# Attention products with v cut into 64x32 tiles that sum in a spare half bank, scores packed on 640 columns, maxima issued ahead of the mask wait

## The chip, the cores and the metric

The kernel runs on one core of one Trainium2 chip. The metric is the device time of one execution in microseconds (us). The kernel before takes 1580.54 us, the median of 3 runs (1578.85 to 1582.73).

The engines are named as in the profile: PE is TensorE's matmul, PEld its weight load, DVE is VectorE, ACT is ScalarE, POOL is GpSimd, SP is SyncE (it issues most DMAs).

## The reference

Four layers are applied in turn to x (2048 rows of 640): attention, feed-forward, attention, feed-forward, with the same weights both times.

```python
def _A_ref(x, wqkv, wo):          # H = 32 heads, Dh = 20, window W = 256
    qkv = (x @ wqkv).reshape(B, S, 3, H, Dh).transpose(2, 0, 3, 1, 4)
    q, k, v = qkv
    scores = einsum("bhqd,bhkd->bhqk", q, k) * Dh ** -0.5
    mask = (i - j >= 0) & (i - j < 256)          # i query, j key
    p = softmax(where(mask, scores, -1e9))
    return einsum("bhqk,bhkd->bhqd", p, v) ... @ wo
def _B_ref(x, w1, b1, w2, b2):
    return relu(x @ w1 + b1) ** 2 @ w2 + b2
x = x + _A_ref(_layernorm(x)); x = x + _B_ref(_layernorm(x))     # twice
```

## The kernel before, in words

**Units.** The rows are cut into blocks of T = 256, so each of the 2 layers has 8 blocks; a block of a layer is a *unit* u, 16 in all. A query of a unit sees keys of its own block and of the one before it. Only units 0 and 8 (the first block of a layer) have no block before.

**Dense work.** The projections to q and k (`stage_qk`), to v (`stage_v`), the output projection (`stage_o`) and the feed-forward (`stage_f`) are chains of 128x128 matmuls, all issued on one line, L327. Every operand is split into two fp16 parts and three of the four products are summed. The moving operand has 256 columns (q, k, first feed-forward matrix) or 320 (v, output, second feed-forward matrix). They accumulate in two buffers of PSUM, `acc` (tag "mm").

**Attention work.** Heads go in groups of four, a *quad*: 8 quads per unit. The four heads of a quad are j = 0, 1 by e = 0, 1. For a quad three things happen on PE:

- *maxima* (`max_quad`, L653): the scores with queries on partitions, 38 matmuls on 64x64 tiles, into `bb`, two PSUM tensors of three banks of 512 columns (e = 0 is bb_133 in the built program, e = 1 is bb_134). They fill columns 0 to 1280 of the 1536. DVE then merges two window ends (COPY_PREDICATED, L666) and takes the row maximum (TENSOR_REDUCE, L669), once for each e. The maxima are turned, by a DMA, into extra rows of q, so that the second set of scores already has its row maximum subtracted.
- *scores* (`exp_quad`, L767): the scores again, keys on partitions, 32 matmuls on 64x64 tiles into the same `bb`. ACT takes their exponential into `pt` (L789), six times 512 columns. POOL sets what the window excludes to zero, eight affine_selects of 128x256 (L804, L808).
- *product with v* (`pv_quad`, L838): pt times v in fp32 on 128x32 tiles, so that the four heads of the quad run side by side, each on its 32 columns of PE; 16 matmuls, each of which the profile shows as two records (x32). A head streams 768 columns (256 + 128 + 128 + 256). The sum lies in an "mm" buffer, and ACT copies it to `ot` (L850), which is stored to DRAM by DMA.

The maxima of a quad run three quads ahead of its scores (LEAD). `bb` is one pair of buffers, so maxima wait for the exponentials that read the scores, and scores wait for the reduction that read the maxima.

**What sets the order.** Each engine runs its instructions in the order in which Python issues them. PE's order comes out of a small planner: it keeps a clock `now` with a cost for each piece of PE work, and a list of jobs for DVE, ACT, POOL and SP with costs and priorities (`urgency`, 0 first), issued when the planned clock gets there. In `together` (L1105 ff.) a unit alternates: scores of quad n, dense work, maxima of quad n + 3 and product of quad n, dense work. `work(part, Want(...))` issues dense work until its share is done and the jobs named in `Want` have ended by the plan. Before the maxima, `Want` names the exponentials and the first masks of quad n (`wants += quad[1][0]`, L1146); then the maxima and the product follow each other directly.

Where a buffer is written and read by different engines, semaphores are set when the program is built. The planner does not know them.

In the steady units (2 to 7 and 9 to 13) the order of PE repeats from unit to unit. `stage_o` of the last unit must wait until the last product has gone to DRAM and come back (`load_o`, `od`); the planner keeps feed-forward work of the unit before for that time (KEEP, CARRY).

Of the kernel before, what the change touches and what calls it, by code (L numbers as in the profile page):

```python
# [45 lines left out]
def kernel(ctx: ExitStack, tc: tile.TileContext, x, wqkv, wo, w1, b1, w2, b2, out):  # L46
# [12 lines left out]
    masks = sb.tile([P, 3 * P], BF16, name="pt", tag="pt", bufs=6)  # L59
# [120 lines left out]
    class Want:  # L180
        def __init__(self, *jobs, bank=True):
            self.jobs, self.bank = [j for j in jobs if j is not None], bank

    def when(w):

        if any(j.end is None for j in w.jobs):
            return None
        t = max([0.0] + [j.end for j in w.jobs])
        if w.bank and len(banks2) > 1:
            free = [max(j.end for j in b) + LAT for b in banks2 if b and all(j.end is not None for j in b)]  # L190
            if not free:
                return None
            t = max(t, min(free))
        return t
# [125 lines left out]
    urgency = {"out": 0, "turn": 1}  # L320
# [134 lines left out]
    def ln_cross(u, *deps):  # L455

        prio = 1 if u == 3 else 2
# [288 lines left out]

    def exp_quad(n):

        u, qd = divmod(n, NQ)
        qt = qts[u]  # L750
        bb = banks()
        whole = not quarters(u) or n == NQ
        steps = steps_of(u)
        if qd % GQ == 0:
            need(rowjobs.pop((u, qd // GQ)))
        pieces = []
        for k, st in enumerate(steps):
            o = 0
            for kb, kt, ko, q0, qn in st:
                w = qn * P  # L760
                for j in range(2):
                    for h in range(0 if whole else 2):
                        a, b = (0, w - 64 * (1 - h)) if kb < 2 else (64 * h, w)

                        def put(e, k=k, kt=kt, ko=ko, q0=q0, j=j, h=h, o=o, a=a, b=b):
                            r, rows = slice(64 * e, 64 * e + 3 * DH + 2), slice(64 * h, 64 * (h + 1))
                            nc.tensor.matmul(bb[e][rows, k, o + a:o + b],  # L767
                                             kt[r, 2 * qd + j, ko + 64 * h:ko + 64 * (h + 1)],
                                             qt[r, 2 * qd + j, q0 * P + a:q0 * P + b], start=True, stop=True,
                                             tile_position=(64 * e, 64 * h))  # L770

                        pieces.append((h, b - a, put))
                    for e in range(2 if whole else 0):
                        r = slice(64 * e, 64 * e + 3 * DH + 2)
                        nc.tensor.matmul(bb[e][:, k, o:o + w], kt[r, 2 * qd + j, ko:ko + P],  # L775
                                         qt[r, 2 * qd + j, q0 * P:q0 * P + w], start=True, stop=True)
                    o += w
        by_tiles(pieces)
        now[0] += (870.0 if whole else 763.0) if u % NG else 530.0
        out, masks = [], []  # L780
        for k, st in enumerate(steps):
            pts, ms = [], []
            for e in range(2):
                o = sum(2 * qn * P for _, _, _, _, qn in st)
                box = {}

                def power(k=k, e=e, o=o, box=box):
                    box["pt"] = sb.tile([P, 512], F32, name="pt", tag="pt", bufs=6)
                    nc.scalar.activation(box["pt"][:, :o], bb[e][:, k, :o], AF.Exp, scale=SCALE / (QS * QS))  # L789

                ex = post("A", 50 + 0.834 * o, power, prio=urgency["turn"])
                bbjobs.append(ex)
                o2 = 0
                for kb, kt, ko, q0, qn in st:
                    w = qn * P
                    part = slice(o2, o2 + 2 * w)
                    o2 += 2 * w

                    def mask(box=box, part=part, kb=kb, w=w):
                        pj = box["pt"][:, part].rearrange("p (j n) -> p j n", j=2)  # L800
                        if kb < 2:

                            m = pj[:, :, w - P:w]
                            nc.gpsimd.affine_select(out=m, in_=m, pattern=[[0, 2], [-1, P]],  # L804
                                                    compare_op=ALU.is_gt, fill=0.0, base=0, channel_multiplier=1)
                        else:
                            m = pj[:, :, 0:P]
                            nc.gpsimd.affine_select(out=m, in_=m, pattern=[[0, 2], [1, P]],  # L808
                                                    compare_op=ALU.is_ge, fill=0.0, base=0, channel_multiplier=-1)

                    ms.append(post("G", 375, mask, ex, prio=0 if n > NQ * NU - 4 else 1))
                    pts.append((e, kb, q0, qn, box, part))
            out.append(pts)
            masks.append(ms)
        return out, masks

    def steps_of(u):

        cur, prev = kts[u % 3], kts[(u - 1) % 3]
        if u % NG == 0:  # L820
            return [[(2, cur, 0, 0, 2)], [(3, cur, P, 1, 1)]]
        return [[(1, prev, P, 0, 2)], [(0, prev, 0, 0, 1), (3, cur, P, 1, 1)], [(2, cur, 0, 0, 2)]]

    def pv_quad(n, quad):
        u, qd = divmod(n, NQ)
        steps = steps_of(u)
        pv, jobs = mm_tile([P, T], "pv")
        for k, pts in enumerate(quad[0]):
            need(*quad[1][k])
            for kb, kt, ko, q0, qn in steps[k]:  # L830
                vf = vts[(2 * (u if kb >= 2 else u - 1) + kb % 2) % 6][1]
                for j in range(2):
                    for e, kb_, _, _, box, part in pts:
                        if kb_ == kb:
                            jj = 2 * j + e
                            c = (4 * qd + jj) * (DH + 1)
                            pj = box["pt"][:, part].rearrange("p (j n) -> p j n", j=2)
                            nc.tensor.matmul(pv[32 * jj:32 * (jj + 1), q0 * P:(q0 + qn) * P],  # L838
                                             vf[:, c:c + 32], pj[:, j, :], start=(k == 0),
                                             stop=(k == len(steps) - 1), skip_group_check=True,  # L840
                                             tile_position=(0, 32 * jj))
            now[0] += 480.0 if u % NG else 400.0
# [6 lines left out]
        def out():  # L849
            nc.scalar.copy(ot[:, qd % 2], pv)  # L850
# [6 lines left out]
        jobs.append(post("A", 262, out, prio=0))  # L857
        if qd % 2:
            ojobs[u, qd] = dma(write, 4 * (DH + 1) * 2 * T * 4, jobs[-1], n=4, cost=350.0)
# [5 lines left out]
    ols = {}  # L865

    def load_o(u, late=False, free_=()):
# [42 lines left out]
        for i in range(4):  # L910
# [15 lines left out]
            pr = 2 if u else 1  # L926
# [4 lines left out]
        ols[u] = od, x1, js, xj  # L931
        if u == 0:
# [371 lines left out]
```

## Time and profile before

| | us |
|---|---|
| median of 3 runs | 1580.54 |
| the profiled execution, its own time | 1585.88 |
| its span, first to last instruction | 1584.2 |
| PE busy | 1555.0 |
| DVE busy | 928.6 |
| ACT busy | 733.5 |
| POOL busy | 607.9 |

The profile is of one execution. A row of groups reads: line, engine, operation, output<-input, partitions x elements, count | busy time, mean ns of one | idle time before it and what ended it. A row of the timeline reads: start (us from the start of the span), length, engine, line, operation, count, and in brackets the idle time before it and its releaser. Lengths of matmul records are modelled and overlap; the difference between two starts is what counts.

### The profile page before, as it was taken

The numbers are of one execution on the slowest core, as the hardware profiler recorded it, in microseconds if no ns is written. First come the engines' busy times: TensorE is split into PE (matmuls) and PEld (weight loads), VectorE is DVE, ScalarE is ACT, GpSimd is POOL, SyncE is SP. The second block draws the span as 40 slices with busy tenths as digits, with TensorE's granted clock in tenths as the row PEclk, the third lists the DMA queues.
The fourth block names the chain that finished last, engine by engine and source line by source line (L and its number), as shares of the span: only waits on it lengthen the run. The fifth ranks groups of instructions, "written<-read, shape, count | busy, mean of one in ns | idle before, by whom it ended". The sixth has DMA issues, their size and how long they took to land.

```text
span 1584.2 us, 51151 instructions
## 1 busy us (share of the span) xinstructions
PE 1555.0 (98%) x21570; PEld 1167.1 (74%) x21570; DVE 928.6 (59%) x1910; ACT 733.5 (46%) x1593; POOL 607.9 (38%) x1291
## 2 busy tenths in 40 slices
PE   8888999999999999999999999999999999999999
PEld 7665778777777777777777777777777777777777
DVE  8776664565655566465465646566465565556542
ACT  4454545345354444534434454444534445445522
POOL 1232535335343352534414253343524435344522
PEclk9999999999999999999999999999999999999999
DMA  9764343352534625345253533525344253441120
GB/s 270 192 175 125 69 116 83 98 115 65 121 80 108 122 50 123 87 106 108 62 138 81 117 91 107 111 54 120 86 120 94 67 132 68 123 90 58 30 65 19
DMA packets 243341, 160.35 MB, mean 101 GB/s; under 512 B 91176, under 2 KB 226856, under 8 KB 243112
## 3 DMA queue, kind: packets, MB, share of 16 engines
q1 hardware_dynamic: 236744, 147.58, 38.6%
q10 hardware_dynamic: 6368, 9.50, 2.0%
q8 instruction: 169, 2.77, 0.8%
q14 instruction: 60, 0.49, 0.1%
HBM read 84.68 MB, written 52.95 MB: 87 GB/s over the span
## 4 chain that ended last, share of the span: by engine, by line
PE 93%; DVE 2%; DMA 2%; ACT 1%; issue 1%; POOL 0%; SPq 0%; ACTq 0%; DVEq 0%; POOLq 0%
PE acc L327 72%; PE pv L838 11%; PE bb L653 5%; PE bb L767 5%; ACT pt L789 1%; DMA x<-in_A_x_dram 1%; PE bb L775 0%; DMA qt<-mT 0%; DVE mx L669 0%; PE bb L678 0%; DVE bb L633 0%; DMA o<-ot 0%; DVE bst L353 0%; DMA xt<-in_A_x_dram 0%; DVE bb L666 0%
## 5 line engine op out<-in xcount | busy, mean ns | idle before, releaser
L789 ACT ACTIVATE pt<-bb 128x512 f32<-128x512 f32 (+1 forms) x736 | 374.0, 600 | 226.0 <-PE bb L767 198.8
L804 POOL TENSOR_SCALAR_AFFINE_SELECT pt<-pt 128x256 f32<-128x256 f32 x448 | 187.2, 420 | 539.7 <-ACT pt L789 525.6
L327 PE MATMUL acc<-y,w_s 128*128 128x256 f16 x2880 | 328.3, 273 | 0.1
L327 PE MATMUL acc<-w_s,hh 128*128 128x320 f16 (+1 forms) x2340 | 326.8, 298 | 0.0
L327 PEld LDWEIGHTS <-w_s 128*128 128x128 f16 x2880 | 276.5, 98 | 51.3 <-issue 15.0
L327 PEld LDWEIGHTS <-hh 128*128 128x128 f16 x2340 | 221.9, 98 | 97.6 <-issue 12.7
L669 DVE TENSOR_REDUCE mx<-bb 128x4 f32<-128x1024 f32 x224 | 273.9, 1223 | 6.6
L327 PEld LDWEIGHTS <-wq_s 128*128 128x128 f16 x2400 | 230.1, 98 | 46.8 <-issue 14.0
L327 PE MATMUL acc<-yT,wq_s 128*128 128x256 f16 x2250 | 258.8, 273 | 2.3 <-DVE qd L510 0.9
L808 POOL TENSOR_SCALAR_AFFINE_SELECT pt<-pt 128x256 f32<-128x256 f32 x512 | 223.1, 458 | 92.3 <-ACT pt L789 91.0
L1023 DVE TENSOR_TENSOR hh<-r,hh 128x256 f16<-128x256 f32 x192 | 94.6, 516 | 225.1 <-ACT hh L1020 218.2
L838 PE MATMUL pv<-pt,vt 128*32 128x128 f32 (+1 forms) x3840 | 189.5, 330 | 0.2 <-POOL pt L804 0.2
L850 ACT COPY ot<-pv 128x256 f32<-128x256 f32 x128 | 47.6, 372 | 286.2 <-PE pv L838 286.2
L1017 POOL TENSOR_TENSOR r<-r 128x256 f32<-128x256 f32 x192 | 114.2, 616 | 157.9 <-ACT r L1013 155.9
L666 DVE COPY_PREDICATED bb<-maskq,bb 128x256 f32<-128x256 uint16 x224 | 93.3, 423 | 98.6 <-PE bb L653 96.8
L327 PE MATMUL acc<-wo_s,od 128*128 128x320 f16 x960 | 140.5, 302 | 3.4 <-DVE od L924 1.9
L838 PEld LDWEIGHTS pv<-pt,vt 128*32 128x32 f32 x3840 | 104.8, 109 | 40.1 <-POOL pt L808 5.5
L327 PE MATMUL acc<-wq_s,yT 128*128 128x320 f16 x900 | 130.6, 300 | 1.4 <-DVE y L378 0.9
L327 PEld LDWEIGHTS <-od 128*128 128x128 f16 x960 | 91.8, 98 | 48.6 <-issue 6.4
L1013 ACT ACTIVATE r<-acc,b1s 128x256 f32<-128x256 f32 x192 | 80.5, 471 | 85.8 <-PE acc L327 84.7
L327 PEld LDWEIGHTS <-yT 128*128 128x128 f16 x900 | 85.5, 98 | 40.7 <-issue 7.8
L364 POOL TENSOR_TENSOR bmv<-bmv,neghalf 128x1 f32<-128x1 f32 x64 | 45.2, 712 | 156.0 <-DVE bmv L358 155.5
(96 smaller groups left out, 1241.6 us busy)
## 6 DMA issues: line engine op xcount, KB each, us to landing
qt<-qk SPq DMA_DIRECT2D x30, 480.0 KB
kt<-qk SPq DMA_DIRECT2D x30, 480.0 KB
qk<-qd SPq DMA_DIRECT2D x17, 640.0 KB
o<-ot SPq DMA_DIRECT2D x256, 42.0 KB
od<-o SPq DMA_DIRECT2D x14, 640.0 KB
qk<-yl SPq DMA_DIRECT2D x13, 640.0 KB
qk<-qd SPq DMA_DIRECT2D x17, 320.0 KB
xt<-in_A_x_dram SPq DMA_DIRECT2D x16, 320.0 KB
```

The source lines that it names most:

```text
L327: nc.tensor.matmul(acc, lhs(a, c), rhs(b, c), start=(k == 0), stop=(k == 3 * nk - 1))
L653: nc.tensor.matmul(flat[e][rows, o:o + b - a], qt[r, p, i * P + 64 * h:i * P + 64 * (h + 1)], kt[r, p, a + to:b + to], start=True, stop=Tr ...
L666: nc.vector.copy_predicated(wins[:, :, 4 * Q:], later, wins[:, :, :Q])
L669: nc.vector.tensor_reduce(most, wins[:, :, Q:], axis=mybir.AxisListType.X, op=ALU.max)
L767: nc.tensor.matmul(bb[e][rows, k, o + a:o + b], kt[r, 2 * qd + j, ko + 64 * h:ko + 64 * (h + 1)], qt[r, 2 * qd + j, q0 * P + a:q0 * P + b] ...
L789: nc.scalar.activation(box["pt"][:, :o], bb[e][:, k, :o], AF.Exp, scale=SCALE / (QS * QS))
L804: nc.gpsimd.affine_select(out=m, in_=m, pattern=[[0, 2], [-1, P]], compare_op=ALU.is_gt, fill=0.0, base=0, channel_multiplier=1)
L808: nc.gpsimd.affine_select(out=m, in_=m, pattern=[[0, 2], [1, P]], compare_op=ALU.is_ge, fill=0.0, base=0, channel_multiplier=-1)
L838: nc.tensor.matmul(pv[32 * jj:32 * (jj + 1), q0 * P:(q0 + qn) * P], vf[:, c:c + 32], pj[:, j, :], start=(k == 0), stop=(k == len(steps) - ...
L1013: nc.scalar.activation(box["r"], acc[:, f, :], AF.Relu, bias=b1s[:, f0 + f:f0 + f + 1], scale=1.0 / (YS * WS))
L1017: nc.gpsimd.tensor_tensor(box["r"], box["r"], box["r"], op=ALU.mult)
L1023: nc.vector.tensor_sub(hh[:, 1, f, :], box["r"], hh[:, 0, f, :])
```

## The change

- **Product with v.** Where a unit has a block before it, keys are now taken in halves of 64 (h = 0, 1). A tile is 64 keys by 32 columns, so eight run side by side. Half h = 0 sums into the upper half of the third bank of e = 0 (`bb6[0][:, 2, 256:]`), half h = 1 into that of e = 1: the 256 columns of `bb` that maxima and scores leave free. A head streams 256 + 128 + 192 + 64 = 640 columns per half. It takes 32 matmuls where there were 16. ACT copies the first sum to `ot`, and a new DVE addition (L872) adds the second.
- **Scores.** They are packed on 640 columns for each j, cut where a bank ends: 38 matmuls for 32. ACT takes four exponentials of 640 columns for six of 512. POOL's eight affine_selects have 64 partitions x 4 x 64 elements for 128 x 2 x 128, and each now waits for both exponentials of its e. `pt` has two buffers of 1280 columns for six of 512.
- **Order.** The masks are no longer in the `Want` ahead of the maxima. After the maxima a second `work` issues dense work until the masks (the last ones up to 600 ns early) and the last product's buffer (`pvfree`) are planned to be ready. Then comes the product.
- **Tables.** `urgency` gets entries that were numbers in the code, other ones from unit 2 on. CARRY goes from 18e3 to 24e3, KEEP from 20e3 to 28e3.

```diff
     def exp_quad(n):
+        return (halves_quad if quarters(u) else whole_quad)(n, u, qd, qt, flat)
...
+    PARTS = [{3: (0, 2, 2), 1: (2, 0, 3), 2: (5, 0, 4), 0: (9, 0, 1)},
+             {3: (0, 3, 1), 1: (1, 0, 4), 2: (5, 1, 3), 0: (8, 0, 2)}]
+    ORDER = [(2, 3, 1, 0), (1, 0, 2, 3)]
...
+            for j in range(2):
+                exps.append(post("A", 584, power(box, flat[e], 10 * Q * j, 10 * Q * (j + 1)), *exps, prio=urgency["exp"]))
+            bbjobs.extend(exps)
+            for at, (k, h) in enumerate(((0, 0), (1, 1), (1, 0), (0, 1))):
+                masks[at // 2].append(post("G", 375, lambda k=k, h=h, mask=mask: mask(k, h), *exps,
...
-        pv, jobs = mm_tile([P, T], "pv")
+        need(*pvfree)
+        pvfree.clear()
+        pv = [b[:, 2, T:] for b in bb6]
...
-                            nc.tensor.matmul(pv[32 * jj:32 * (jj + 1), q0 * P:(q0 + qn) * P],
-                                             vf[:, c:c + 32], pj[:, j, :], start=(k == 0),
-                                             stop=(k == len(steps) - 1), skip_group_check=True,
-                                             tile_position=(0, 32 * jj))
+                        nc.tensor.matmul(pv[h][32 * jj:32 * (jj + 1), q0 * Q:(q0 + w) * Q], vf[r, c:c + 32],
+                                         boxes[e]["pt"][r, a:b], start=(k == 0), stop=(k == (3 if halves else 1)),
+                                         skip_group_check=True, tile_position=(h * Q, 32 * jj))
...
-            nc.scalar.copy(ot[:, qd % 2], pv)
+            nc.scalar.copy(ot[:, qd % 2], pv[0])
+
+        def both():
+            nc.vector.tensor_tensor(ot[:, qd % 2], pv[1], ot[:, qd % 2], op=ALU.add)
...
-            if kind == "v":
-                wants += quad[1][0]
-            work(part, Want(*wants, bank=kind == "v"))
+            work(part, Want(*wants, bank=False))
...
             if kind == "v":
+                work(part, Want(*pvfree, bank=False, soon=[(j, 0.0) for j in quad[1][0]] + [(j, 600.0) for j in quad[1][-1]]))
                 pv_quad(what[1], quad)
...
-    QKC, VC, OC, FCST, LNC, CARRY, KEEP, MID = 16.4e3, 8.2e3, 8.2e3, 39.2e3, 1.2e3, 18e3, 20e3, 10e3
+    QKC, VC, OC, FCST, LNC, CARRY, KEEP, MID = 16.4e3, 8.2e3, 8.2e3, 39.2e3, 1.2e3, 24e3, 28e3, 10e3
```

What the built programs hold at three places follows. A name in brackets after "waits" is the engine whose semaphore the instruction waits for (DVE_49 is DVE's).

*PE, fourth quad of unit 4.* Before: the last maxima, then the product with v.

```order
L653 MATMUL bb_133<-kt_86,qt 64x192
L653 LDWEIGHTS qt
L653 MATMUL bb_134<-kt_86,qt 64x192
L838 MATMUL pv<-pt,vt_89 32x256 [waits Activation_49,Pool_49]
L838 MATMUL pv<-pt,vt_89 32x256 [waits Pool_49]
L838 MATMUL pv<-pt,vt_89 32x256 x2
```

After, at the same place:

```order
L653 MATMUL bb_134<-kt_86,qt 64x192
L327 LDWEIGHTS yT
L327 MATMUL acc<-wq_s,yT 128x320
L327 LDWEIGHTS yT
L327 MATMUL acc<-wq_s,yT 128x320
L327 LDWEIGHTS yT
L327 MATMUL acc<-wq_s,yT 128x320
L858 MATMUL bb_133<-pt,vt_90 32x256 [waits DVE_49,Pool_49]
L858 MATMUL bb_134<-pt,vt_89 32x256 [waits Pool_49]
```

Three dense matmuls have come between maxima and product, and the product, which now writes `bb`, waits for DVE as well. The value waited for is that of the TENSOR_REDUCE on bb_133 in the next piece.

*DVE at the same place.* Before: merge and maximum of e = 0, then of e = 1.

```order
L510 SCALAR_TENSOR_TENSOR yl<-acc,yl 128x256 [waits Activation_49]
L666 COPY_PREDICATED bb_133<-maskq,bb_133 128x4x64 [waits PE_49,Activation_49]
L669 TENSOR_REDUCE mx<-bb_133 128x4 [waits DVE_49]
L666 COPY_PREDICATED bb_134<-maskq,bb_134 128x4x64 [waits PE_49,Activation_49]
L669 TENSOR_REDUCE mx<-bb_134 128x4 [waits DVE_49]
```

After:

```order
L510 SCALAR_TENSOR_TENSOR yl<-acc,yl 128x256 [waits Activation_49]
L666 COPY_PREDICATED bb_133<-maskq,bb_133 128x4x64 [waits PE_49,Activation_49]
L669 TENSOR_REDUCE mx<-bb_133 128x4 [waits DVE_49]
L666 COPY_PREDICATED bb_134<-maskq,bb_134 128x4x64 [waits PE_49,Activation_49]
L872 TENSOR_TENSOR ot<-bb_134,ot 128x256 [waits DVE_49,Activation_49]
L669 TENSOR_REDUCE mx<-bb_134 128x4
```

The first merge and maximum were issued ahead of the product, so the product waits for them; the merge of e = 1 was issued behind it and waits for the product (its PE_49 is a value of L858). The new addition stands between it and its maximum.

*DVE, first quad of unit 4*, where maxima and product still follow each other. Before:

```order
L914 RECIPROCAL rs<-rs 128x64 [waits DMAHW1_49]
L666 COPY_PREDICATED bb_133<-maskq,bb_133 128x4x64 [waits PE_49]
L669 TENSOR_REDUCE mx<-bb_133 128x4 [waits DVE_49]
L666 COPY_PREDICATED bb_134<-maskq,bb_134 128x4x64 [waits PE_49]
L669 TENSOR_REDUCE mx<-bb_134 128x4 [waits DVE_49]
```

After:

```order
L666 COPY_PREDICATED bb_133<-maskq,bb_133 128x4x64 [waits DVE_49,Activation_49]
L666 COPY_PREDICATED bb_134<-maskq,bb_134 128x4x64 [waits DVE_49,PE_49]
L941 TENSOR_TENSOR od<-od,rs 128x5x64 [waits DMAHW2_49,DVE_49]
L872 TENSOR_TENSOR ot<-bb_134,ot 128x256 [waits DMAHW7_49,DMAHW0_49,DVE_49]
L669 TENSOR_REDUCE mx<-bb_133 128x4
L510 SCALAR_TENSOR_TENSOR qd<-acc,qd 128x2x256 [waits Activation_49]
L669 TENSOR_REDUCE mx<-bb_134 128x4
```

Both merges now wait until the product is done: the first for ACT's copy of it (L869, through Activation_49), the second for its last matmul.

Counted over the whole changed program, 65 of the 112 products on halves have dense work between themselves and the matmuls on `bb` ahead of them (before: 3 of 112); in 59 of these those matmuls are the maxima of another quad on halves. Of the 59, 37 products wait for the maximum of e = 0, 21 for merges, and one for the maximum of e = 1. In 47 the product follows the maxima directly. PE changes between kinds of tile 724 times, before 665 times.

175 lines of the change are left out of this document (93 added, 82 removed).

## Prediction

> **What bounds the kernel now.** I read the page first, then the busy time by window, then the timeline of one quad.
>
> ```profile
> span 1584.2 us, 51151 instructions
> PE 1555.0 (98%) x21570; PEld 1167.1 (74%) x21570; DVE 928.6 (59%) x1910; ACT 733.5 (46%) x1593; POOL 607.9 (38%) x1291
> ```
>
> ```profile
> 495.00:594.00 99.00, 99.00 (x1452) 74.38 (x1445) 58.58 (x106) 45.61 (x99) 39.01 (x84) 1.00 0.42 95
> ```
>
> The window's columns after its length are PE, PEld, DVE, ACT, POOL, granted clock, DMA. PE is busy for all of it at full clock. So PE's stream is the time: a microsecond taken out of it, or a wait put into it, reaches the end. DVE, ACT and POOL count only where PE waits for them. The quad shown in the order pieces, in the timeline (engines PE, DVE, ACT):
>
> ```profile
> 440.09 0.75 PE L767 MATMUL bb<-qt,kt 62*64 62x192 f16 x32
> 440.78 1.26 PE L327 MATMUL acc<-yT,wq_s 128*128 128x256 f16 x10
> 441.88 3.83 PE L327 MATMUL acc<-wq_s,yT 128*128 128x320 f16 x27
> 445.64 0.76 PE L653 MATMUL bb<-kt,qt 60*64 60x256 f16 x38
> 446.33 1.51 PE L838 MATMUL pv<-pt,vt 128*32 128x256 f32 x32
> 446.51 0.43 DVE L666 COPY_PREDICATED bb<-maskq,bb 128x256 f32<-128x256 uint16 x1 [3.60 <-PE bb L653]
> 446.98 1.22 DVE L669 TENSOR_REDUCE mx<-bb 128x4 f32<-128x1024 f32 x1
> 447.77 0.58 PE L327 MATMUL acc<-wq_s,yT 128*128 128x320 f16 x3
> 447.93 0.37 ACT L850 COPY ot<-pv 128x256 f32<-128x256 f32 x1 [3.17 <-PE pv L838]
> 448.12 0.42 DVE L666 COPY_PREDICATED bb<-maskq,bb 128x256 f32<-128x256 uint16 x1
> 448.57 1.23 DVE L669 TENSOR_REDUCE mx<-bb 128x4 f32<-128x1024 f32 x1
> ```
>
> From start to start: scores 0.69 us (to 440.78), maxima 0.69 (to 446.33), product 1.44 (to 447.77), a 256-column matmul 1.10/10 = 0.11. The end of the span gives 320 columns:
>
> ```profile
> 1512.75 14.84 PE L327 MATMUL acc<-w_s,hh 128*128 128x320 f16 x108
> 1525.58 0.49 DVE L924 TENSOR_TENSOR od<-ov,od 128x320 f16<-128x320 f32 x1
> 1527.43 2.75 PE L327 MATMUL acc<-wo_s,od 128*128 128x320 f16 x19
> ```
>
> 14.68/108 = 0.136. Twenty-seven of those take 3.67, but 441.88 to 445.64 is 3.76: a change of tile shape costs 0.09 to 0.10.
>
> **The change, part by part.**
>
> *The product's stream.* 1280 fp16 columns per tile (scores) at 0.11/256 a column are 0.55 of 0.69, so some 0.14 are fixed. The product's 768 columns then take 1.30, 1.69 ns each; 640 take 1.08, and the product 1.22. It saves 0.22; 112 times, 24 us. No eight tiles run in this trace, so both ends: if all of the 1.44 goes by columns the gain is 0.24 (27 us); if the short last step of 64 columns takes as long as one of 128, 0.11 (12 us). I take 24, since the maxima show 38 matmuls of 64 to 256 columns on four tiles in 0.69, as long as the scores' 32. The same rows price the scores' 38 matmuls at nothing.
>
> *One more change of shape.* 724 changes for 665: 59 times 0.095 is 5.5 us lost.
>
> *ACT, POOL, priorities.* Four exponentials for six, and a DVE addition per quad (256 columns; the merge of that size takes 0.42), lie off PE's path. They matter through the waits below.
>
> *A wait put in: the product waits for the maxima.* Before, product and maxima lie in different buffers: the product starts at 446.33 while DVE has yet to merge. Now the product writes the third bank of the same `bb`, and the program makes it wait for DVE's work on `bb` that was issued ahead of it. That scores wait for these reductions, and what it costs PE, can be seen here:
>
> ```profile
> 124.78 1.22 DVE L669 TENSOR_REDUCE mx<-bb 128x4 f32<-128x1024 f32 x1
> 126.05 0.75 PE L767 MATMUL bb<-qt,kt 62*64 62x192 f16 x31 [1.24 <-DVE mx L669]
> ```
>
> PE stands for 1.24 us and starts 0.05 after the reduction. In the quad above, counted from the start of the maxima (445.64), the maximum of e = 0 ends at 448.20, 2.56 later, so a product that waits for it starts at 2.61. PE gets there at 0.69 + dense work + 0.10:
>
> - 12 products have three 320-column matmuls (0.41) ahead: there at 1.20, wait 1.41; 16.9 us.
> - 20 have five of 256 or four of 320 (0.55): 1.34, wait 1.27; 25.4 us.
> - 10 have fifteen of 256 and wait for the second merge too (448.54, 2.90): 2.44 against 2.95; 5.1 us.
> - 10 have four of 320 and wait for both merges, which come first (about 1.7): 0.4 each; 4 us.
> - the 7 left: some 3 us.
>
> That is 54 us with DVE free at once. It isn't always:
>
> ```profile
> 469.71 0.76 PE L653 MATMUL bb<-kt,qt 60*64 60x256 f16 x38
> 469.89 2.28 DVE L1023 TENSOR_TENSOR hh<-r,hh 128x256 f16<-128x256 f32 x4 [5.14 <-ACT hh L1020]
> 472.09 0.42 DVE L666 COPY_PREDICATED bb<-maskq,bb 128x256 f32<-128x256 uint16 x1
> ```
>
> Here the merge began 2.38 after the maxima, not 0.87, because four feed-forward steps stood ahead. Some 20 of the quads above lie in that stretch; at a third of those 1.5 us it adds up to 10. I take 60, between 50 and 80. Queued behind the waiting product are all dense matmuls, and behind them everything.
>
> Row first, rule second: in the order of the changed program the product, which writes columns 1280 to 1536, waits for a reduction that reads only up to 1280. The Trainium skill (PSUM — Partial Sum Buffer, "PSUM bank collisions raise a hardware error") says that two engines must not touch one bank in the same 32 partitions at a time, whatever the columns, and asks for semaphores by bank. By that rule the wait cannot be dropped while pv shares the bank; were the guard by column, the 60 us would be 0 and the change a gain.
>
> *A wait moved: the scores after the product.* In the 47 quads where the product follows the maxima, DVE's merges now wait for the product and ACT's copy. The copy ended at 448.30, 1.97 after the product's start; with a product 0.22 shorter, 1.75. Then merge 0.47, merge 0.45, addition 0.45, maximum 1.14, maximum 1.23 (starts 446.51, 446.98, 448.12, 448.57): 5.5 after the product's start. In a steady unit the next scores arrive after the product and 28 (320 columns), 25 + 8 (256 and 320), 30 (320) or 45 (256) dense matmuls, at 5.1, 5.2, 5.4 and 6.3: waits of 0.4, 0.35, 0.1 and 0, about 0.9 a unit. Other DVE work stands in between (the last order piece: L941, then L510):
>
> ```profile
> L510 DVE SCALAR_TENSOR_TENSOR qd<-acc,qd 128x512 f16<-128x512 f32 (+1 forms) x54 | 32.4, 599 | 59.4 <-ACT qd L507 59.1
> L917 DVE TENSOR_TENSOR od<-od,rs 128x320 f32<-128x320 f32 x56 | 30.7, 563 | 1.3 <-DMA od<-o 1.2
> L949 DVE SCALAR_TENSOR_TENSOR x<-acc,x 128x320 f32<-128x320 f32 x60 | 29.4, 491 | 49.6 <-PE acc L327 45.2 <-DMA x<-in_A_x_dram 3.7 <-DMA qt<-mt 0.7
> ```
>
> With one or two of these 0.5 to 0.6 us pieces per quad it is up to 3.3 a unit. Twelve units: 11 to 40 us; I take 24.
>
> *What goes.* The product's own waits for masks:
>
> ```profile
> PEld pv L838 <- POOL pt L808: 5.5, 26, 0.4
> ```
>
> A product that is held for DVE finds its masks done: 5 us back. Maxima that need not wait for masks save nothing more: PE did dense work in that time anyway.
>
> *The tail.* Before, 108 matmuls cover the last product's way to DRAM and back: it ends at 1512.75, the second step of `od` at 1526.07, 13.3 later, and PE comes at 1527.43. The changed program has 88 there (12.0 us) and an addition more (0.45): 13.8 against 12.0, 1.8 us lost.
>
> **Sum.** -24 + 5.5 + 60 + 24 - 5 + 1.8 = +62 on the profiled execution's 1585.9 (its span and 1.7 us around it): 1648. That execution is 5.3 over the median of the three runs, 1580.54; the same 62 on the median give 1643.
>
> **Rivals.**
>
> *1. The waits are covered, and the change is faster.* The mechanism: planner and chip differ so that the product comes to `bb` after DVE has finished. The point is the arrival: from 2.6 us after the maxima on, the product does not wait for the first maximum. Then -24 + 5.5 - 5 + 1.8 = -22, about 1559. For it: the planner puts the product where the masks are due, and if masks come later than I think (POOL has eight selects per quad, 420 to 458 ns each by the rows below), the wait is theirs, not DVE's, and was there in part before. Against it: the matmuls between maxima and product are counted in the program, and only one to three groups' worth of PE time fits; nothing else can hold PE there without being a wait itself. Chance 0.10.
>
> ```profile
> L804 POOL TENSOR_SCALAR_AFFINE_SELECT pt<-pt 128x256 f32<-128x256 f32 x448 | 187.2, 420 | 539.7 <-ACT pt L789 525.6
> L808 POOL TENSOR_SCALAR_AFFINE_SELECT pt<-pt 128x256 f32<-128x256 f32 x512 | 223.1, 458 | 92.3 <-ACT pt L789 91.0
> ```
>
> *2. The eight tiles do not overlap.* If the two halves of keys ran one after the other, a product would take 2 x 1.08 + 0.14 = 2.3, 0.86 more than now: +96 for -24, and 1763. Against it: the maxima already run row halves (e) side by side. Less sharply, records could have a least spacing. The forecast needs 64 records in 1.08 us, 17 ns apart; the maxima show 38 in at most 0.69, 18 ns, with time to spare for columns. Chance 0.03. The Trainium skill (TensorE: Matmul & The Clock Gate, "Wait — 56ns, not 53.3ns?") gives a floor of about 25 ns between starts; by that the product would be 1.6 + 0.14 and the sum 1701, but the maxima's 38 in 0.69 lie under that floor here.
>
> *3. Gains and waits cancel.* Half of the waits would have to vanish at once, and nothing in the rows does that. Chance 0.03.
>
> **How the numbers follow.** The forecast (waits for DVE on `bb`) has 0.84, and 1643. Its own ends: product stream -27 to -12, product waits 50 to 80, score waits 11 to 40, the rest +2: +36 to +110, of which the corners are unlikely together. I give 1604 to 1682 (+24 to +101); that leaves out rival 1, rival 2 and the corners. About 0.3% (4.7 us) is what a measurement of this kernel can tell from no change. Faster 0.10 (rival 1), the same 0.03 (rival 3), slower 0.87 (forecast and rival 2).
>
> **What would show it.** In the profile of the changed kernel the list of waits should have PE's product (L858, PE or PEld) waiting for DVE L669 and L666, about 60 us in some 55 waits, and scores (L782) waiting for DVE L669, 10 to 40 us. The product should go from its first to the next group in 1.22 us where nothing holds it. A steady unit should take about 5 us more than before, where the chain of waits meets the same fifty matmuls every 96.57 us:
>
> ```profile
> 404.25 5.57 PE acc L327 x50
> 500.82 5.56 PE acc L327 x50
> ```
>
> The forecast is wrong if PE stays at 98% with a product of 1.22 (rival 1), or if the product itself takes over 1.44 (rival 2).

## The result, and the profile after

The changed kernel takes 1715.51 us, the median of four runs (1713.78 to 1717.38), against 1580.24 before (also four runs, one more than above): a ratio of 1.0854, 95% interval 1.0836 to 1.0873. It is slower, as forecast, but by 135 us where 62 were forecast, and it lies above the range. The profiled execution has a span of 1715.4 us, 131.2 more than the one before.

First the page of the changed kernel, then the same window as in the prediction, with the same columns (length, PE, PEld, DVE, ACT, POOL, granted clock, DMA):

```profile
span 1715.4 us, 59505 instructions
PE 1581.0 (92%) x25842; PEld 1217.7 (71%) x25842; DVE 962.4 (56%) x2022; ACT 670.8 (39%) x1369; POOL 644.1 (38%) x1291
```

```profile
495.00:594.00 99.00, 92.76 (x1614) 71.72 (x1615) 53.35 (x103) 39.09 (x78) 37.55 (x78) 1.00 0.40 95
```

PE was busy for all of these 99 us before; now it stands for 6 of them. What it stands for is in the list of waits (engine, line, what it waited for: us in total, times, the longest). From it the rows of PE that concern the attention part and its accumulators:

```profile
PE bb L858 <- DVE mx L669: 50.3, 36, 2.2
...
PE bb L858 <- DVE bb L666: 20.0, 14, 1.7
...
PE acc L327 <- DVE qd L510: 10.5, 12, 1.3
...
PE bb L858 <- POOL pt L795: 8.7, 13, 1.3
...
PE bb L782 <- DVE mx L669: 8.0, 21, 1.8
```

The product's wait for DVE is there, 70 us in 50 waits (60 in some 55 were forecast). So is that of the scores. The third row, dense matmuls that wait for DVE to empty an accumulator, was in no term of the forecast. The list counts only idle time between records, whose lengths are modelled; from start to start, as below, the product's waits come to 84 us and those of the scores to 21.

Two starts of the product show a steady unit, first quad to first quad, 105.48 us for 96.57:

```profile
542.21 1.37 PE L858 MATMUL bb<-pt,vt 64*32 64x256 f32 x64
```

```profile
647.69 1.37 PE L858 MATMUL bb<-pt,vt 64*32 64x256 f32 x64
```

The forecast had 5 us a unit; 8.9 came.

### The profile page after: what moved, and what is told of

The parts are those of the page before. It is cut to its first block, busy times and chain, and to the rows that moved or that the text cites. A ratio compares the mean times of both kernels' runs of the same rounds, so it can differ in the third digit from the quotient of the medians.

```text
span 1715.4 us, 59505 instructions
## 1 busy us (share of the span) xinstructions
PE 1581.0 (92%) x25842; PEld 1217.7 (71%) x25842; DVE 962.4 (56%) x2022; ACT 670.8 (39%) x1369; POOL 644.1 (38%) x1291
## 5 line engine op out<-in xcount | busy, mean ns | idle before, releaser
L795 POOL TENSOR_SCALAR_AFFINE_SELECT pt<-pt 64x256 f32<-64x256 f32 x896 | 406.4, 454 | 595.0 <-ACT pt L767 544.8
L767 ACT ACTIVATE pt<-bb 128x640 f32<-128x640 f32 (+2 forms) x512 | 310.4, 685 | 250.3 <-PE bb L782 226.5
L327 PE MATMUL acc<-y,w_s 128*128 128x256 f16 x2880 | 335.4, 274 | 0.9 <-DVE y L378 0.9
L327 PE MATMUL acc<-w_s,hh 128*128 128x320 f16 (+1 forms) x2340 | 331.9, 299 | 2.0 <-DVE hh L1051 2.0
L858 PE MATMUL bb<-pt,vt 64*32 64x192 f32 (+4 forms) x7424 | 185.7, 313 | 85.4 <-DVE mx L669 50.3
L858 PEld LDWEIGHTS bb<-pt,vt 64*32 64x32 f32 (+1 forms) x7424 | 144.8, 109 | 129.9 <-POOL pt L795 95.4
L1051 DVE TENSOR_TENSOR hh<-r,hh 128x256 f16<-128x256 f32 x192 | 99.3, 549 | 201.2 <-ACT hh L1048 197.8
L869 ACT COPY ot<-bb 128x256 f32<-128x256 f32 x128 | 47.6, 372 | 395.9 <-PE bb L858 389.1
L327 PE MATMUL acc<-wq_s,yT 128*128 128x320 f16 x900 | 134.3, 302 | 12.7 <-DVE qd L510 10.5
L782 PE MATMUL bb<-qt,kt 62*64 62x64 f16 (+3 forms) x4256 | 96.4, 222 | 11.8 <-DVE mx L669 8.0
L782 PEld LDWEIGHTS <-kt 62*64 62x64 f16 x4256 | 72.3, 107 | 44.4 <-issue 40.8
```

The lines of the kernel that those rows point to most:

```text
L327: nc.tensor.matmul(acc, lhs(a, c), rhs(b, c), start=(k == 0), stop=(k == 3 * nk - 1))
L767: return lambda: nc.scalar.activation(room_of(box)[:, a:b], bank[:, a:b], AF.Exp, scale=SCALE / (QS * QS))
L782: nc.tensor.matmul(flat[e][h * Q:(h + 1) * Q, c0:c1], kt[r, 2 * qd + j, k0:k0 + Q], qt[r, 2 * qd + j, q:q + c1 - c0], start=True, stop=Tru ...
L795: nc.gpsimd.affine_select(out=m, in_=m, pattern=[[0, 4], [-1 if k else 1, Q]], base=0, fill=0.0, compare_op=ALU.is_gt if k else ALU.is_ge, ...
L858: nc.tensor.matmul(pv[h][32 * jj:32 * (jj + 1), q0 * Q:(q0 + w) * Q], vf[r, c:c + 32], boxes[e]["pt"][r, a:b], start=(k == 0), stop=(k == ...
L869: nc.scalar.copy(ot[:, qd % 2], pv[0])
```

## The experiments

A time without more is the median of the kernel's own runs; each ratio is to runs of the kernel before on the same chip. Where a sum "from start to start" is given, it goes over all starts of PE's matmuls in the profiled execution: what lies between two starts beyond the usual distance of such a pair is a wait. The usual distance is a choice, so such sums are good to some 5 us. The time of a unit runs to its first product from that of the unit before it.

**e1, the order alone.**

```diff
-            if kind == "v":
-                wants += quad[1][0]
-            work(part, Want(*wants, bank=kind == "v"))
+            work(part, Want(*wants, bank=False))
...
             if kind == "v":
+                work(part, Want(bank=True, soon=[(j, 0.0) for j in quad[1][0]] + [(j, 600.0) for j in quad[1][-1]]))
                 pv_quad(what[1], quad)
```

> The kernel before with one part of the change: maxima no longer wait for the masks, a second stretch of dense work stands behind them, then the product. The product keeps its 128x32 tiles and its own mm buffer. Theory A (the loss comes from sharing bb between DVE's maxima and the product): no wait for DVE here, some 28 more changes of tile kind, 1577 to 1592 us. Theory B (the loss comes from the order itself, the product reaching masks that are not ready): 1620 us or more.

1583.76 us, ratio 1.0013 (0.9997 to 1.0030): no difference. PE is as busy as before:

```profile
PE 1553.9 (98%) x21570; PEld 1164.8 (74%) x21570; DVE 930.5 (59%) x1910; ACT 733.5 (46%) x1593; POOL 607.6 (38%) x1291
```

Theory B (the order by itself) falls. But the planner puts dense work between maxima and product in only a quarter of the quads here, so this kernel says little on what masks cost in the changed one.

**e2, the numbers alone.**

```diff
+        if u == 2:
+            urgency.update({"out": 0, "od": 1.5, "cross": 0.5, "mask": 0.5, "turn": 0.5, "exp": 0.5, "ln": 0.5, "y": 0.5})
...
-    ... 18e3, 20e3, 10e3
+    ... 24e3, 28e3, 10e3
```

> The kernel before with the change's numbers alone: the priorities of urgency with their other values from unit 2 on, KEEP, CARRY, and the Want that goes with them. Theory A (sharing bb is the cause): no difference or little, 1570 to 1590 us. Theory C (the priorities slow DVE, ACT and POOL): 1595 us or more.

1579.97 us, ratio 0.9982 (0.9972 to 0.9992): level with the kernel before, or faster by 0.2%, which is less than the 0.3% that the prediction took as the least that can be told from no change. By themselves the priorities are no part of the loss. No other version in the study that computes everything comes under the kernel before.

**e3 and e8, the old order put back.** Both take the second `work` out and let the maxima wait for masks again; e3 for the first masks, e8 for all.

```diff
+            if kind == "v":
+                wants += [*quad[1][0], *pvfree]                  # e3
+                wants += [*quad[1][0], *quad[1][1], *pvfree]     # e8
             work(part, Want(*wants, bank=False))
...
-                work(part, Want(*pvfree, bank=False, soon=...))
```

> The changed kernel with the old order back: maxima wait for the masks, the product stands directly behind them. Theory A: the product finds DVE at rest on bb and its start waits (84 us) go, with them some 6 us of tile changes; but DVE's merges now stand behind the product in all quads, so the waits of scores and dense work grow from some 36 to between 40 and 80 us: 1630 to 1670 us. Theory B (masks): the masks are awaited by dense work again, all waits go, 1570 to 1590 us. Theory C (the packed scores, larger exponentials and priorities slow DVE, ACT and POOL): 1690 us or more.

1753.15 us, ratio 1.1074 (1.1027 to 1.1121). That lies in the range of theory C, but C is not the cause: e2 has its priorities, and e5 below has its packed scores and, half of them uncut, its larger exponentials; both take 1580 us. The timeline of PE in one of its quads shows what had been overlooked:

```profile
541.89 0.76 PE L653 MATMUL bb<-kt,qt 60*64 60x256 f16 x38
542.58 0.88 PE L858 MATMUL bb<-pt,vt 64*32 64x256 f32 x32
545.37 0.67 PE L858 MATMUL bb<-pt,vt 64*32 64x192 f32 x32 [1.90 <-DVE mx L669]
```

The product stands in the middle. While the planner passes time for the second half of the masks it issues DVE's maximum, and the second half of the product, issued after it, has to wait for it. e3 does not take the wait away, so it could not decide what it was made for. e8 was made to.

> The changed kernel with the old order, as e3_maxima_wait_again, but the maxima wait for all masks, so that by the built program no product waits for DVE, at its start or inside (in e3 the planner let DVE's reductions in between the two halves of the masks, and products stood for them). Theory A: product waits for DVE 0 and for masks under 10 us; in turn DVE's merges stand behind the product and ACT's copy in all quads: by the dense matmuls that follow the product here, scores come 3.7 to 5.9 us after its start where the reductions need 5.5, 5 us of waits a unit, and accumulators are emptied late (some 25 us): 1640 to 1690 us. Theory B (only the masks hold the changed kernel): 1570 to 1600 us.

1804.37 us, ratio 1.1418 (1.1401 to 1.1435), above the ranges of both theories. No product on halves waits for DVE's maxima any more, and theory B falls with 1570 to 1600. That the wait turns round, as theory A had it, was right; its size was not. The waits:

```profile
DVE bb L666 <- ACT ot L869: 356.4, 108, 9.2
...
PE bb L782 <- DVE mx L669: 75.5, 110, 2.2
```

In 108 quads DVE's merge stands behind ACT's copy of the product, and 110 times the scores stand for DVE's maximum. From start to start the scores wait 107 us (5 a unit, some 70 in all, were expected; the changed kernel has 23), maxima another 26 for the exponentials, and from unit 14 to the last product it takes 63 us longer than before.

**e4 and e5, the third bank without maxima.** Both leave the first 64 keys of each window out of the maxima, so that these lie in the first two banks and the product alone with the scores' last columns in the third. They differ in one thing: in e5 that bank is a PSUM tensor of its own.

```diff
-                p, at = 2 * qd + j, 5 * Q * w
-                cuts = sorted({0, 5 * Q, *(z - at for z in (512, 1024) if 0 < z - at < 5 * Q)})
+                p, at = 2 * qd + j, 4 * Q * w
+                cuts = [0, 4 * Q]
...
-                    nc.vector.copy_predicated(wins[:, :, 4 * Q:], later, wins[:, :, :Q])
+                    pass
```

and for e5 as well

```diff
-    bb6 = [ps.tile([P, 3, 512], F32, name=f"bb{e}") for e in range(2)]
+    bb6 = [(ps.tile([P, 1024], F32, name=f"ba{e}"), ps.tile([P, 512], F32, name=f"bc{e}")) for e in range(2)]
...
-        pv = [b[:, 2, T:] for b in bb6]
+        pv = [b[1][:, T:] for b in bb6]
```

> The changed kernel, but its maxima leave out the first 64 of each window's 320 keys and the merge, so that maxima and DVE's reductions use the first two banks of bb alone and the product the third; same PSUM tensors, same order. Theory A1 (the wait is made for a bank): no wait of the product for DVE is left; product waits only for masks (some 20 us), scores and dense work wait little: 1585 to 1610 us. Theory A2 (the wait is made for the whole PSUM tensor): the waits stay, shorter by the merge (0.45 us): 1635 to 1665 us. Theory B (masks): 1680 us or more. The maxima stream a fifth less, 11 us, which is in all numbers.

> As e4_maxima_two_banks (first 64 of 320 keys of each window left out of the maxima), and the third bank of each e is declared as a PSUM tensor of its own; exponentials that cross into it are cut in two. Theory A1 (bank) gives the same time as e4_maxima_two_banks within 10 us. Theory A2 (tensor): the waits of the product for DVE and of DVE for the product go only here, 1585 to 1610 us, 30 us or more under e4_maxima_two_banks. Theory B (masks): 1680 us or more.

e4: 1636.46 us, ratio 1.0346 (1.0316 to 1.0377). e5: 1580.33 us, ratio 0.9996 (0.9979 to 1.0013). Theory A2 had 1635 to 1665 and 1585 to 1610, at least 30 apart: the first is met, the second came 5 us under its range, and the two lie 56 apart. Theories A1 and B fall. Of e4 the waits of PE, and of e5 (whose product is L865, its scores L789):

```profile
PE bb L858 <- DVE mx L669: 26.3, 24, 1.8
PE bb L858 <- POOL pt L795: 17.1, 24, 1.8
PE bb L782 <- DVE mx L669: 8.7, 12, 1.8
```

```profile
PE bc L865 <- POOL pt L802: 1.8, 3, 0.9
...
PE ba L789 <- DVE mx L672: 0.9, 2, 0.5
...
PE acc L327 <- DVE qd L510: 0.4, 1, 0.4
```

In e4 no maximum touches the product's bank, and the product still waits for it. In e5 it doesn't, and with it go the waits of scores and of dense matmuls. Its timeline has the two side by side:

```profile
437.47 1.23 DVE L672 TENSOR_REDUCE mx<-ba 128x4 f32<-128x1024 f32 x1 [3.48 <-PE ba L656]
437.80 1.37 PE L865 MATMUL bc<-pt,vt 64*32 64x256 f32 x64
```

So the wait is made for the tensor as it is declared, not for the bank: 56 us between two kernels that differ in the declaration (and in exponentials cut in two). The declaration alone would not do for the change itself, whose maxima reach to column 1280 and so into the third bank: in e4 and e5 they stop at 1024.

e5 also gives an estimate of what the change would be without the wait. Its maxima stream 13 us less than those of before (0.575 for 0.688 in 112 quads), and its time is the same: with whole maxima, and DVE's merges left out as they are, it would be some 11 us slower than before. By that the shared tensor makes some 124 of the 135 us. From start to start the product has lost its 16 us, but products stand 32 us inside themselves, where before they stood 7: masks. In the steady units this is the fifth and the sixth quad. The fifth of unit 4 in e5, on POOL and PE:

```profile
446.57 1.95 POOL L802 TENSOR_SCALAR_AFFINE_SELECT pt<-pt 64x256 f32<-64x256 f32 x4
448.61 1.23 POOL L1052 TENSOR_TENSOR r<-r 128x256 f32<-128x256 f32 x2
449.79 2.17 POOL L802 TENSOR_SCALAR_AFFINE_SELECT pt<-pt 64x256 f32<-64x256 f32 x4
...
449.96 2.71 PE L865 MATMUL bc<-pt,vt 64*32 64x256 f32 x64
```

Two steps of the feed-forward (L1052) stand between the first four selects and the last four, and the product, there at 449.96, ends only behind the last select (451.96).

**e6, masks at their true cost.**

```diff
-                exps.append(post("A", 584, power(...
+                exps.append(post("A", 690, power(...
...
-                masks[at // 2].append(post("G", 375, ...
+                masks[at // 2].append(post("G", 460, ...
...
-                ... [(j, 600.0) for j in quad[1][-1]]
+                ... [(j, 0.0) for j in quad[1][-1]]
```

> e5_third_bank_own_tensor (own PSUM tensor for the third bank, first 64 of 320 keys of each window left out of the maxima), but the planner prices an exponential at 690 ns and a select at 460 (584 and 375 in the change) and no product is let go 600 ns ahead of its last masks. Theory M1 (the 32 us that products of e5 stand inside themselves are masks that the planner thinks earlier than they are): these waits fall under 10 us, some 35 more changes of tile kind cost 3: 1555 to 1567 us. Theory M2 (POOL is behind in any case): 1573 us or more.

1590.51 us, ratio 1.0061 (1.0040 to 1.0082): worse than e5, in the range of M2, and 22 us of waits inside the products are left. M1 was wrong, at least as the main cause. That fits POOL's own queue, as in the quad of e5 above; an order in which the feed-forward's steps come behind the selects was not tried.

**e7, dense work for the waits.**

```diff
+            if kind == "s":
+                wants += pvfree
...
-                work(part, Want(*pvfree, bank=False, soon=...
+                work(part, Want(*pvfree, *bbjobs, bank=False, soon=...
...
-    SHARE = 0.55
+    SHARE = 0.35
```

> The changed kernel, whole computation, same PSUM tensors, but the planner is told of the waits: the product is planned behind the reductions of the maxima (bbjobs), the scores behind ACT's copy and DVE's addition (pvfree), the true costs of exponentials and selects, SHARE 0.35 for 0.55 so that dense work is left for both places. Theory A (84 us of product waits, 36 of score and dense waits, 13 of masks, all for want of dense work at the right place): each kind of wait falls under 10 us; the product's gain of 16 and some 100 changes of tile kind at 0.1 remain: 1572 to 1592 us. Theory D (PE has too little dense work between two quads, the wait only moves to another place): 1620 us or more.

1656.94 us, ratio 1.0480 (1.0463 to 1.0498): 59 us of the 135 are back, and the time lies in the range of theory D. The mechanism of theory A shows all the same where there is enough dense work. One quad of its timeline:

```profile
1186.81 0.76 PE L653 MATMUL bb<-kt,qt 60*64 60x256 f16 x38
1187.50 5.61 PE L327 MATMUL acc<-w_s,hh 128*128 128x320 f16 x40
1193.04 1.37 PE L858 MATMUL bb<-pt,vt 64*32 64x256 f32 x64
1194.34 1.26 PE L327 MATMUL acc<-w_s,hh 128*128 128x320 f16 x8
1195.53 0.76 PE L782 MATMUL bb<-qt,kt 62*64 62x128 f16 x38
```

Nothing waits here: 5.5 us of dense work stand where DVE reduces, 1.2 where ACT copies and DVE adds. Units 11 to 13 take 97.1 us, 0.5 over before. But units 3 to 7 take 101.6, with 3 to 4 us of waits inside products. Most of that is one quad a unit, the second: its product comes 2.83 us after the start of the maxima, does not wait at its start, but stands inside itself for DVE's maximum of e = 1. And where dense work is short, in unit 1 (15 us over before) and from unit 15 to the last product (25), theory D holds.

**f1, f2, f3, in search of a faster version.** All compute everything and have the third bank as a tensor of its own. f1 puts the first 64 keys of the maxima there (the product then waits for the merges alone) and plans for it as e7 does. f2 goes back to the old order and puts half h = 0 into an `mm` buffer:

```diff
-        pv = [b[:, 2, T:] for b in bb6]
+        pvm, jobs = mm_tile([P, T], "pv")
+        pv = [pvm, bb6[1][1][:, T:]]
```

f3 lets DVE do merge and maximum of e = 0, the addition, then merge and maximum of e = 1:

```diff
-                j = post("D", 330, merge, prio=urgency["turn"])
+                j = post("D", 330, merge, *([bbjobs[-1]] if e else []), prio=urgency["turn"])
...
-        pvfree.append(post("D", 330, both, left, prio=0) ...
+        pvfree.append(post("D", 330, both, left, *bbjobs[-2:-1], prio=0) ...
```

> The changed kernel, whole computation: third bank as a PSUM tensor of its own, which holds the first 64 keys of the four windows of the maxima (so the product waits for DVE's merges alone, and both merges go ahead of the maxima), planner told of merges, copy and addition and of the true costs, SHARE 0.4. Theory A: no kind of wait over 10 us; product 16 less, some 105 changes of tile kind 10 more: 1566 to 1585 us. Theory D (the wait only moves): 1600 us or more.

> Whole computation, 64x32 tiles and packed scores of the change. Half h = 0 of the product goes to an mm buffer, half h = 1 beside the maxima's heads (first 64 keys of the windows) in the third bank of e = 1, the third banks being PSUM tensors of their own; the product directly behind the maxima as before the change (masks awaited ahead; in the last two units the changed order), KEEP and CARRY as before. By the built program no product waits for DVE's maxima. Theory A: the product's 16 us are gained, changes of tile kind as before (674 for 665), waits of scores, dense work and masks together within 10 us of those of before: 1560 to 1576 us. Theory C (larger exponentials, one more DVE addition or POOL hold it back in any case): 1582 us or more.

> f2_halves_mm_and_own with DVE's work in the order in which it can run: merge and maximum of e = 0 (which need nothing of the product), the addition, merge and maximum of e = 1; the changed order now also in unit 1, masks 800 ns ahead for 400. In f2 a steady unit took 97.0 us, with 1.1 us of waits of scores and accumulators for DVE, and unit 2 took 8 us more than before. Theory A (DVE held by the product was what remained): steady units 95.6 to 96.3, unit 2 under 100, 1572 to 1590 us in all. Theory C (larger exponentials and POOL hold it back in any case): steady units 96.6 or more, 1593 us or more.

f1 1610.03 (ratio 1.0179, 1.0149 to 1.0210), f2 1600.89 (1.0126, 1.0108 to 1.0145), f3 1595.23 (1.0095, 1.0073 to 1.0117): all above what theory A expected, and in the ranges of the other theories (D for f1, C for f2 and for the time of f3). f1 pays 12 us in changes of tile kind and dense stream and some 15 more than before in waits inside products. f3's steady units take 96.43 us, between the two theories, a shade under before (96.57) and level with e2 (96.39). From start to start the product is 1.02 shorter a unit, but the scores are 0.76 longer, since DVE's last maximum still comes late, and the maxima 0.1. What f3 loses, it loses in units 1 and 2 (3.4 us) and from unit 15 to the last product (13), where dense work is short.

## Why the prediction was right or wrong

The side was right, and so was the main mechanism: the product, writing `bb`, waits for DVE. e5 shows it by taking it away. The sum was half of the truth, and most of what it lacked lies in three steps. The product's waits for DVE came to 84 us for 60, mainly because the products that wait for both merges were priced at 0.4 and stood 1.8. The masks were booked as 5 us back, and the waits inside the product grew by 13. And dense matmuls that wait behind the product had no term and took 20. From start to start, changed against before, in us (the rows are rounded):

| term | forecast | measured |
|---|---|---|
| stream of the product | -24 | -16 |
| changes of tile kind, dense stream | +5.5 | +10 |
| product waits at its start, units 1 to 15 | +60 | +84 |
| waits inside the product (masks; half clock) | -5 | +13 |
| scores wait | +24 | +21 |
| dense matmuls wait | 0 | +20 |
| the rest, tail and unit 0 included | +1.8 | 0 |
| sum | +62 | +131 |

*The stream of the product.* Where nothing holds it a product takes 1.30, not 1.22. Three of the four steps go by columns as assumed (0.455 for 256, 0.219 for 128, 0.325 for 192); the last, 64 columns with the way out, takes 0.302 where the forecast's 1.22 would leave 0.222. That was the other end in the text ("if the short last step of 64 columns takes as long as one of 128"), and the gain lies nearer to it. Rival 2 falls: eight tiles overlap.

*Product waits.* The step that failed here is "10 have four of 320 and wait for both merges, which come first (about 1.7): 0.4 each; 4 us". Each of them stood about 1.8. The seventh quad of unit 4, on POOL, DVE and PE:

```profile
514.01 2.03 POOL L795 TENSOR_SCALAR_AFFINE_SELECT pt<-pt 64x256 f32<-64x256 f32 x3
...
516.01 0.54 POOL L364 TENSOR_TENSOR bmv<-bmv,neghalf 128x1 f32<-128x1 f32 x1
516.59 0.80 DVE L366 TENSOR_SCALAR xt<-xt,bmv 128x640 f32<-128x640 f32 x1 [1.30 <-POOL bmv L364]
...
517.31 0.74 DVE L666 COPY_PREDICATED bb<-maskq,bb 128x256 f32<-128x256 uint16 x2
...
517.87 1.40 PE L858 MATMUL bb<-pt,vt 64*32 64x256 f32 x42 [1.74 <-DVE bb L666]
```

A small step of a layer norm (L364) stands behind selects on POOL; DVE waits for it at L366; the merges stand behind L366, and the product behind the merges. Eleven such quads, one in each steady unit, cost 20 us for 4. The quads with three dense matmuls wait 1.53 (1.41 forecast), those with fifteen 0.60 (0.51), and those with five of 256 in the stretch of the feed-forward 1.75 (1.27, with 10 us set aside for DVE's other work). Units 1, 14 and 15 came out about as forecast; unit 0 added 5 us that nobody forecast (they are in the last row).

*Masks.* "A product that is held for DVE finds its masks done: 5 us back" failed. From start to start the last masks of the sixth quad of a steady unit come 0.44 us after its product's start, and the product stands inside itself for 0.31 (the seventh stands as long for the merge of e = 1); nine products at half clock, below, add some 9 us. And e5 suggests that more was hidden behind DVE's wait: without it products stand 25 us longer inside themselves than before.

*What stands behind the product on DVE.* I followed DVE's chain to the next scores and stopped there. It also holds what empties the accumulators. DVE and PE after the first quad of unit 5:

```profile
544.07 0.76 DVE L666 COPY_PREDICATED bb<-maskq,bb 128x256 f32<-128x256 uint16 x2 [1.59 <-ACT ot L869]
...
545.14 0.42 DVE L872 TENSOR_TENSOR ot<-bb,ot 128x256 f32<-128x256 f32 x1
545.47 1.22 DVE L669 TENSOR_REDUCE mx<-bb 128x4 f32<-128x1024 f32 x1
546.60 0.68 DVE L510 SCALAR_TENSOR_TENSOR qd<-acc,qd 128x512 f16<-128x512 f32 x1
```

```profile
547.34 1.25 PE L327 MATMUL acc<-wq_s,yT 128*128 128x320 f16 x8 [0.93 <-DVE qd L510]
```

DVE stood 1.59 for ACT's copy of the product; L510 came behind the maximum; the dense matmuls stood 0.93 for L510. Eleven units have this wait, 12 us from start to start (the list of waits has 10.5); most of the other 8 us are dense matmuls at half clock, below. No term had either. The scores themselves waited 21 more, near the 24.

*The guard.* The text took the wait to follow PSUM's banks and brought in the Trainium skill (PSUM — Partial Sum Buffer, "PSUM bank collisions raise a hardware error") for it. e4 against e5 says otherwise for this program: the wait follows the declared tensor. The rule itself is neither shown nor refuted, since in e5 the two engines are in different banks. The sentence "the wait cannot be dropped while pv shares the bank" was true in effect, since the maxima of the change reach into that bank. The way out that the text did not see was to keep the maxima, or all of them but what is merged early, out of a third bank declared as a tensor of its own; f1 to f3 go that way and still do not beat the kernel before.

Rival 1 had asked whether the product reaches `bb` after DVE has finished; that needs 2.6 us after the start of the maxima. In e7 the products that come 2.83 us after it do not wait at their start: the distance was right, but the changed program does not have it.

## To carry to other kernels

Before a spare corner of a buffer is used, ask which waits its declaration brings, in both directions, and who stands behind each waiter on its engine: a reduction that nobody waited for became the bound for PE, and a copy that nobody waited for became the bound for DVE. Follow the queue behind a waiting instruction to its end, accumulators and POOL's small steps included, not only to the next consumer that the change names. And price a shorter stream step by step: the last short step did not go by its columns.

## What the hardware did that was not expected

PE's clock falls after such waits. A product of the changed kernel that stood 1.69 us, what follows it on PE, and the windows of 1 us there (the granted clock is the third figure from the end):

```profile
489.61 2.39 PE L858 MATMUL bb<-pt,vt 64*32 64x256 f32 x64 [1.69 <-DVE mx L669]
491.93 4.00 PE L327 MATMUL acc<-y,w_s 128*128 128x256 f16 x30
```


```profile
488.00:489.00 1.00, 0.00 (x0) 0.00 (x0) 0.97 (x2) 0.00 (x0) 0.85 (x3) 1.00 0.00 0
489.00:490.00 1.00, 0.39 (x9) 0.32 (x17) 0.46 (x1) 0.00 (x0) 1.00 (x2) 0.84 0.00 0
490.00:491.00 1.00, 1.00 (x40) 0.89 (x32) 0.00 (x0) 0.00 (x0) 0.37 (x1) 0.50 0.00 0
491.00:492.00 1.00, 1.00 (x40) 0.81 (x25) 0.00 (x0) 0.00 (x0) 0.00 (x0) 0.50 0.00 0
492.00:493.00 1.00, 1.00 (x6) 0.69 (x7) 0.80 (x3) 0.37 (x1) 0.00 (x0) 0.50 0.00 0
493.00:494.00 1.00, 1.00 (x10) 0.90 (x9) 1.00 (x2) 0.73 (x2) 0.18 (x1) 0.95 0.06 16
```

At half clock for 3.4 us this product took 2.32 for 1.30. Between 200 and 1560 us there are ten such stretches, 17 us of clock lost in all; in the kernel before and in e5 there is none. In the steady units 9 of the 22 products that stood 1.75 us or more were followed by one, and none of the eleven that stood 1.5 to 1.6. Part of the masks' and the dense matmuls' rows in the table above is this. The mean granted clock goes with the waits: 0.997 before, 0.987 changed, 0.972 in e3, 0.960 in e8. The Trainium skill (TensorE: Matmul & The Clock Gate, "What's actually happening") has the clock halve after an idle window of about 3.4 us that runs freely; the length of the stretch agrees, but gaps of half that length were enough here, now and then.

What decides can be read from the clock's records in the trace. The ten stretches are each 3.41 us long and start at 411.18, 489.68, 701.31, 807.12, 1028.99, 1134.80, 1213.31, 1319.12, 1452.24 and 1503.44. The distances are whole multiples of 3.413 (23, 62, 31, 65, 31, 23, 31, 39 and 15 times), so that the execution can be laid out in intervals of that length. Of the 22 products that stood 1.75 us or more, ten stood within one interval, and nine of these were followed by half clock from its end on; twelve were cut by the border of two intervals, and none of these was. Ten of the eleven that stood 1.5 to 1.6 did so within one interval without harm. So here a wait costs clock when it takes more than about half of one interval, and a shorter one, or one that falls across a border, does not; which of them it will be is luck of the position. Where exactly the limit lies stays open, since one product that stood 1.76 us within an interval (unit 2) was not followed by half clock.

Matmuls on different tiles start very close: the eight records of one step of a product start within 47 ns, and its 64 within 1.15 us. The floor of about 25 ns between starts, which the prediction cited from the Trainium skill (TensorE: Matmul & The Clock Gate, "Wait — 56ns, not 53.3ns?"), does not hold across tiles here: 64 records would need 1.6.
